# One hand-listed order for three batches of attention and two groups of the MLP, with casts of k on ScalarE

## The chip, the cores and the metric

The kernel runs on one core of a Trainium2 chip. The metric is the device time of one execution in microseconds (us).

## The reference

```python
def _attn_ref(q, k, v):                      # q, k, v: (8, 12, 448, 64) float32
    scores = (1 / sqrt(64)) * q @ k^T
    attn = np.maximum(scores, 0.0) ** 2 / S
    return attn @ v

def _moe_ref(x, w_in, w_out):                # x: 3584 x 768 = attention's output
    h = x @ w_in                             # 768 x 2048
    g = h * (1.0 / (1.0 + np.exp(-1.702 * h)))
    return g @ w_out                         # 2048 x 768
```

## The kernel before

Four heads of one batch are a unit u (three units a batch, 24 in all). One score step makes a 128 x 896 block in PSUM (the memory that TensorE's products are written to, here used in eight banks), ScalarE takes the relu, VectorE squares it; seven steps later an attention product uses the squares and VectorE evicts it into x transposed (xt). Tokens are taken in eight groups; m1 is one product of a group with 128 columns of w_in (six matmuls, followed by the gelu on ScalarE and a cast on GpSimd), m2 is a plain product with w_out. From group 1 on, products with w_out are made in pairs of token blocks from sums of the operands (seven products in place of eight); the sums of w_out that this needs are made once, on VectorE.

```python
    def relu2(u, j, sc):
        rl = rlp.tile([128, 2, S], F16, name="rl", tag="rl")
        at = atp.tile([128, 2, S], F16, name="at", tag="at")
        if NP <= u < 2 * NP and j == 3:
            nc.vector.tensor_scalar(out=rl, in0=sc[:, :, 0:S], scalar1=0.0, ..., op0=ALU.max)
        else:
            nc.scalar.activation(out=rl, in_=sc[:, :, 0:S], func=AF.Relu)
        if defer[0]:
            pend.append((at, rl))            # squared later, one per m1 or pair (flush)
        else:
            nc.vector.tensor_tensor(out=at, in0=rl, in1=rl, op=ALU.mult)
        return at
    ...
        # pair(): a product's bank "op", and its eviction
        elif n == 1:
            product(A[1][1], w_c, op)
            evac(eb, op, None)                                   # ScalarE
            nc.vector.tensor_tensor(out=ec, in0=ea, in1=eb, op=ALU.add)
        elif n == 2:
            product(sums[5], wout[1][1], op)
            evac(o0[:, hi], op, ea)                              # VectorE, frees the bank
            nc.vector.tensor_tensor(out=ea, in0=ec, in1=o0[:, hi], op=ALU.subtract)
    ...
        for f in range(NF):                  # group 0
            m1(0, f)
            ...
            if f % 2 == 1 or f > 12:
                visit(min(3, b1 - pos[0]))   # three steps: scores, or an attention product
        ...
            while prepped[0] < min(NU, upto_prep):
                cast(prepped[0], "k", nc.vector)
                cast(prepped[0], "q", nc.gpsimd)
                trans(prepped[0])
        ...
        for m in range(gblk[0] // 2):
            m2(0, m, 0)
            ...
            for i in range(4):               # four sums of w_out after each m2
                ...
                weight_sum(o, x, y, op, i, nc.vector)
```

All products and the sums' evictions share two PSUM banks (the other six hold scores and attention products), so a bank whose eviction is late stops TensorE two products on (for 1.43 us at 129.45 us, the longest such wait of the kernel before).

## Time and profile before

| | kernel before |
|---|---|
| time, median of 4 (range) | 399.82 us (399.57 to 400.13) |
| span of the profiled execution | 398.7 us |
| first product of group 0 (f0) starts | 30.41 us |
| first product of group 2 (g2) starts | 113.42 us |

The two marks cut the kernel where the argument needs it: up to f0 there is attention of batch 0 alone, between f0 and g2 lies what the list orders, and after g2 both kernels run the same schedule, whose casts and pair evictions the change alters. In all views PE is TensorE, PEld its weight loads, DVE VectorE, ACT ScalarE and POOL GpSimd; L292 is line 292 of that kernel, and `ht<-xt,win` reads output<-inputs. The marks can be read off TensorE's timeline (start, duration, engine, line, operation, output and inputs, shape, count):

```profile
30.41 0.82 PE L292 MATMUL ht<-xt,win 128*128 128x384 f16 x4
...
113.42 2.12 PE L292 MATMUL ht<-xt,win 128*128 128x384 f16 x12
```

The page's first part gives each engine's busy us, share and instructions. TensorE's 94% makes it the bound, but not evenly, as the stretches in the prediction show.

```profile
PE 372.9 (94%) x3104; PEld 194.0 (49%) x3104; DVE 267.6 (67%) x429; ACT 216.4 (54%) x317; POOL 145.0 (36%) x200
```

### The profile page before, as it was taken

To read this page: it belongs to the slowest core of one execution; us is meant where nothing else is said; L and a number is where in the kernel's file an instruction comes from. 1 tells how busy PE (TensorE), PEld (TensorE's weight loads), DVE (VectorE), ACT (ScalarE), POOL (GpSimd) and SP (SyncE) were. 2 spreads that over 40 slices of the span, in tenths; PEclk is the share of its full clock that TensorE was granted. 3 is DMA by queue.
4 is the path that set the end of the run, shared out by engine and by line. 5 is a ranking of instruction groups with operands and counts; after the bars stand their busy time and mean duration, and the time that the engine had idled before them with its cause. 6 is when DMAs were issued, how large, how long until landed. Compare 5 with 4: busy or idle time off the path is not lost.

```text
span 398.7 us, 7806 instructions
## 1 busy us (share of the span) xinstructions
PE 372.9 (94%) x3104; PEld 194.0 (49%) x3104; DVE 267.6 (67%) x429; ACT 216.4 (54%) x317; POOL 145.0 (36%) x200
## 2 busy tenths in 40 slices
PE   6588999999998999999999998999999999999994
PEld 3343545344454555454455554454545555554552
DVE  2886676678879688576877778566767765124484
ACT  3885671477775465666565564466666651232200
POOL 8444425534566142332453142333332222223100
PEclk9969999999999999999999999999999999999999
DMA  8999996999696725992969644971240111210323
GB/s 122 197 205 205 204 274 133 231 181 216 137 193 106 206 45 147 224 141 62 150 156 147 169 100 88 221 172 52 49 102 24 41 39 26 55 42 0 79 81 80
DMA packets 65222, 50.85 MB, mean 128 GB/s; under 512 B 35745, under 2 KB 61729, under 8 KB 65185
## 3 DMA queue, kind: packets, MB, share of 16 engines
q1 hardware_dynamic: 47872, 35.70, 38.2%
q0 software_dynamic: 17152, 14.55, 24.6%
q8 instruction: 24, 0.39, 0.4%
q10 hardware_dynamic: 160, 0.10, 0.1%
q14 instruction: 14, 0.11, 0.1%
HBM read 45.61 MB, written 11.01 MB: 142 GB/s over the span
## 4 chain that ended last, share of the span: by engine, by line
PE 68%; DVE 17%; ACT 5%; issue 4%; DMA 3%; POOL 1%; SPq 0%; DVEq 0%; ACTq 0%; POOLq 0%
PE ht L292 28%; PE op L358 24%; PE av L181 7%; PE sc L143 7%; ACT rl L157 4%; DVE at L171 3%; DVE osb L369 3%; PE op L319 3%; DVE at L161 2%; DVE k L104 2%; DMA qst<-in_q_dram 1%; DVE gt L353 1%; DVE wsum L343 1%; DMA q<-in_q_dram 1%; DVE as L353 1%
## 5 line engine op out<-in xcount | busy, mean ns | idle before, releaser
L299 POOL TENSOR_SCALAR gt<-gf 128x384 f16<-128x384 f32 (+1 forms) x128 | 90.8, 710 | 212.1 <-ACT gf L297 210.2
L157 ACT ACTIVATE rl<-sc 128x896 f16<-128x896 f32 x165 | 146.1, 920 | 37.3 <-PE sc L143 34.1
L292 PE MATMUL ht<-xt,win 128*128 128x384 f16 (+1 forms) x768 | 162.2, 353 | 2.9 <-DVE xt L198 1.0
L297 ACT ACTIVATE gf<-ht 128x384 f32<-128x384 f32 (+1 forms) x128 | 70.0, 547 | 114.5 <-PE ht L292 105.8
L292 PEld LDWEIGHTS <-win 128*128 128x128 f16 x768 | 71.8, 98 | 76.9 <-issue 16.5
L171 DVE TENSOR_TENSOR at<-rl 128x896 f16<-128x896 f16 x126 | 81.2, 670 | 13.6 <-ACT rl L157 13.3
L143 PE MATMUL sc<-qT,kT 64*64 64x448 f16 x672 | 49.4, 365 | 8.4 <-DVE qT L133 3.3
L358 PEld LDWEIGHTS <-gt 128*128 128x128 f16 x408 | 39.1, 98 | 33.0 <-issue 7.2
L358 PEld LDWEIGHTS <-as 128*128 128x128 f16 x312 | 30.1, 98 | 23.9 <-issue 3.8
L358 PE MATMUL op<-wout,as 128*128 128x384 f16 x224 | 40.7, 326 | 0.8 <-DVE osb L369 0.8
L358 PE MATMUL op<-wsum,gt 128*128 128x384 f16 x224 | 40.7, 326 | 0.3 <-ACT gf L297 0.3
L181 PE MATMUL av<-at,v 64*64 64x448 f16 x672 | 38.0, 360 | 3.0 <-DVE at L171 2.0
L143 PEld LDWEIGHTS <-kT 64*64 64x64 f16 x672 | 18.2, 106 | 34.7 <-issue 23.2
L358 PE MATMUL op<-wout,gt 128*128 128x384 f16 (+1 forms) x184 | 32.4, 319 | 2.7 <-DVE osb L369 2.1
L198 DVE CAST xt<-av 128x768 f16<-128x768 f32 (+2 forms) x36 | 26.9, 776 | 11.1 <-PE av L181 11.0
L161 DVE TENSOR_TENSOR at<-rl 128x896 f16<-128x896 f16 x42 | 25.9, 624 | 11.3 <-ACT rl L157 11.0
L181 PEld LDWEIGHTS <-v 64*64 64x64 f16 x672 | 20.7, 109 | 15.8 <-issue 5.4
L369 DVE SCALAR_TENSOR_TENSOR osb<-op,osb 128x384 f32<-128x384 f32 (+1 forms) x23 | 12.4, 541 | 23.3 <-PE op L358 23.0
L353 DVE TENSOR_TENSOR as<-gt 128x1024 f16<-128x1024 f16 x36 | 28.0, 804 | 0.0
L401 DVE TENSOR_TENSOR osb<-ea,eb 128x384 f32<-128x384 f32 x11 | 8.2, 743 | 23.7 <-ACT eb L367 23.7
L91 POOL DMA_DIRECT2D v<-in_v_dram x24 | 17.9, 745 | 8.4 <-DMA win<-in_moe_w_in_dram 2.9
L104 DVE CAST k<-kst 128x896 f16<-128x896 f32 x18 | 18.1, 1006 | 0.0
(38 smaller groups left out, 192.0 us busy)
## 6 DMA issues: line engine op xcount, KB each, us to landing
out_dram<-osb SPq DMA_DIRECT2D x54, 192.0 KB, 2.9
kst<-in_k_dram SPq DMA_DIRECT2D x18, 448.0 KB, 4.1
qst<-in_q_dram SPq DMA_DIRECT2D x18, 448.0 KB, 5.2
v<-in_v_dram POOLq DMA_DIRECT2D x24, 224.0 KB, 4.8
win<-in_moe_w_in_dram POOLq DMA_DIRECT2D x8, 384.0 KB, 11.3
wout<-in_moe_w_out_dram POOLq DMA_DIRECT2D x4, 768.0 KB, 11.7
k<-in_k_dram POOLq DMA_DIRECT2D x6, 224.0 KB, 9.0
q<-in_q_dram POOLq DMA_DIRECT2D x6, 224.0 KB, 8.9
```

The lines of the kernel that those rows point to most:

```text
L104: eng.tensor_copy(out=o, in_=i)
L143: nc.tensor.matmul(out=sc[c, a, 0:S], lhsT=st["kT"][r, j, c], rhs=st["qT"][r, :, c], start=True, stop=True)
L157: nc.scalar.activation(out=rl, in_=sc[:, :, 0:S], func=AF.Relu)
L161: nc.vector.tensor_tensor(out=at, in0=rl, in1=rl, op=ALU.mult)
L171: nc.vector.tensor_tensor(out=at, in0=rl, in1=rl, op=ALU.mult)
L181: nc.tensor.matmul(out=st["av"][64 * a:64 * a + 64, s, 0:S], lhsT=st["v16"][r, a, 64 * j:64 * j + 64], rhs=at[r, a, :], start=(j == 0), st ...
L198: nc.vector.tensor_copy(out=xts[g][:, 2 * pr:2 * pr + 2, 64 * (lo - gcum[g]):64 * (hi - gcum[g])], in_=av[:, :, 64 * (lo - b * J):64 * (hi ...
L292: nc.tensor.matmul(out=ht[:, 0:n], lhsT=w[:, kk, fo:fo + 128], rhs=xts[g][:, kk, 0:n], start=(kk == 0), stop=(kk == NK - 1))
L297: nc.scalar.activation(out=gf[:, 0:n], in_=ht[:, 0:n], func=AF.Gelu_apprx_sigmoid, scale=1.0 / SC)
L299: nc.gpsimd.tensor_scalar(out=gts[g][:, f, 0:n], in0=gf[:, 0:n], scalar1=SC, scalar2=1.0, op0=ALU.mult, op1=ALU.mult)
L353: nc.vector.tensor_tensor(out=out_, in0=x, in1=y, op=op)
L358: nc.tensor.matmul(out=op[:, 0:cw], lhsT=lhs[:, f, :], rhs=w[:, f, c0:c0 + cw], start=(start and f == 0), stop=(stop and f == HF - 1))
```

## The change

The loops that built the first 113 us are replaced by one list of words: `s3.4` is a score step, `a3` an attention product, `f0` and `F0` products of groups 0 and 1, `m0`, `n0` the two halves of group 0's output products, `e2` "square until two are left", `B2`, `A2` ... single sums of w_out, `K6`, `Q6`, `R6` casts and transposes, `L6`, `W6` loads, `d` a relu on VectorE, `h` one held until the next product. Batch 0's first attention product goes to the two product banks. Casts of k move from VectorE to ScalarE everywhere. In the pairs, three sums made from SBUF give way to two second evictions of the same bank.

```diff
-            t, u, j = items[pos[0]]
 ...
+        words = (
+            "e2 e1 s0.0 s0.1 e0 q1 s0.2 e1 s0.3 s0.4 k1 e2 e2 s0.5 k2 e0 e0 s0.6 s1.0 a0m "
 ... (13 lines cut)
+            "D2 e3 e0 e0 e2 F14 D3 e1 D1 e0 F15 e1 W12 e0 e0 L12").split()
 ...
-                cast(prepped[0], "k", nc.vector)
+                cast(prepped[0], "k", nc.scalar)
 ...
-            nc.vector.tensor_tensor(out=ec, in0=ea, in1=eb, op=ALU.add)
         elif n == 2:
             product(sums[5], wout[1][1], op)
             evac(o0[:, hi], op, ea)
-            nc.vector.tensor_tensor(out=ea, in0=ec, in1=o0[:, hi], op=ALU.subtract)
+            evac(o0[:, lo], op, eb, sc=-1.0 / SC)
         elif n == 3:
             product(sums[2], wout[0][0], op)
             evac(o1[:, lo], op, eb)
-            nc.vector.tensor_tensor(out=eb, in0=ec, in1=o1[:, lo], op=ALU.subtract)
+            evac(o1[:, hi], op, ea, sc=-1.0 / SC)
```

## The prediction

Its sum stands at 2.0 + 4.8 + 2.5 = 9.3 us, with the 0.83 us for a cast of k on ScalarE estimated from five relus of the kernel before (4.16 us). Where the text speaks of contention, the trace of the kernel before has four sums at 3.42 us beside a cast of q on GpSimd and the next four, without one, at 1.95, and three squares at 3.54 us from 104.44 us, beside casts on GpSimd, but three at 1.69 from 86.14 us, with nothing on GpSimd. Four more sums took 1.95 us from 72.94 us beside GpSimd's casts of the gelu, so not every operation there goes with longer times; that GpSimd is the cause was the author's reading.

> **What bounds the kernel now.** I read the stretches first, to see which engine is full when, then TensorE's timeline with its gaps, then the chain of work around single gaps, then the durations by form. The first view gives, for each stretch in us from the start of the span, busy us (and instruction counts) of TensorE, its weight loads, VectorE, ScalarE and GpSimd, the granted clock, the DMA share and GB/s.
>
> ```profile
> core 0: us, PE busy (x) PEld busy (x) DVE busy (x) ACT busy (x) POOL busy (x), PEclk, DMA share, GB/s
> 4.00:30.40 26.40, 18.96 (x290) 10.02 (x288) 19.64 (x34) 19.17 (x23) 16.07 (x24) 0.87 1.24 198
> 30.40:62.70 32.30, 28.69 (x316) 14.55 (x313) 21.73 (x33) 20.59 (x32) 12.14 (x20) 1.00 1.17 218
> 62.70:77.00 14.30, 13.39 (x74) 6.93 (x71) 10.14 (x18) 2.28 (x4) 8.63 (x9) 1.00 0.95 177
> 77.00:113.40 36.40, 35.14 (x313) 16.36 (x312) 25.95 (x39) 27.32 (x38) 18.05 (x23) 1.00 0.89 187
> 113.40:335.00 221.60, 216.35 (x1793) 113.78 (x1790) 163.14 (x257) 132.19 (x197) 76.31 (x100) 1.00 0.55 115
> 335.00:393.00 58.00, 57.14 (x323) 31.12 (x321) 26.36 (x48) 13.36 (x24) 10.94 (x18) 1.00 0.18 48
> ```
>
> The first row is attention of batch 0 alone: no product of group 0 can start before it, and TensorE is 72% busy there. The next three rows are group 0, then its first output products beside the sums of w_out, then group 1. ScalarE works 2.28 us in the 14.3 us of the third: no scores are made there, so it stands still while VectorE makes sums. From 113.4 us on TensorE is 98% busy. The kernel is therefore TensorE-bound from 30 us on; what can be won is TensorE's idle time (7.4 us before 30.4, 5.7 from there to 113.4, 5.3 to 335) and work the pipeline does at a worse rate.
>
> TensorE's timeline after 113 us has six gaps of note; three of them, with the chain of work (start, length) ahead of one:
>
> ```profile
> 129.45 1.46 PE L358 MATMUL op<-wout,gt 128*128 128x384 f16 x8 [1.43 <-DVE osb L369]
> 193.12 1.46 PE L292 MATMUL ht<-xt,win 128*128 128x512 f16 x6 [0.55 <-DVE osb L369]
> 241.69 0.38 PE L181 MATMUL av<-at,v 64*64 64x448 f16 x4 [1.71 <-DVE at L171]
> ```
> ```profile
> 186.62 0.57 DVE osb L369
> ...
> 187.22 0.56 DVE ea L405
> 187.78 0.60 DVE as L353
> 188.38 1.48 DVE at L171 x2
> 189.86 1.79 DVE k L104
> 191.65 0.95 DVE at L171
> 192.60 0.48 DVE osb L369
> ```
>
> Here a PSUM bank waits for its eviction, which stands in VectorE's queue behind a sum for ea, two squares, and a cast of k that took 1.79 us. The six gaps are 0.29, 1.43, 0.53, 0.55, 0.28 and 1.71 us, 4.8 us together, and five of them have VectorE's backlog as their cause.
>
> [...]four sums of w_out beside a GpSimd cast of q took 3.42 us, the next four without one 1.95; the k cast is 0.61 us at its shortest and 1.01 on average. [...]The trace has 0.92 for the relu from PSUM, [...]back to back, five relus took 4.16 us, 0.83 each, so I count 0.83 of queue time. [...]TensorE was 38% busy from 16 to 20 us, and the granted clock was 0.50 from 20 to 26 us.
>
> **Part 1, batch 0 (start to f0, the first product of group 0).** Nothing is removed; the transposes come in another order, squares are placed singly, and the first attention product goes to the two product banks, so that it does not hold a score bank. ScalarE sets the pace: relus begin at 8.07 us, f0 needs 21 of them, 21 x 0.83 = 17.4, so 25.5 us, then a square (0.54 start to start), the last step of the attention product (0.4) and the larger eviction (0.7): 27.1 us at best. VectorE has 21 squares x 0.54, 8 copies x 0.54 and three evictions x 1.1 = 19.0 us from 6.1 us, so 25.1, just under it. Before, f0 began at 30.41, of which the half-clock stretch cost some (ScalarE idle 1.68 us ahead of 24.59). I take 28.4: a gain of **2.0 us**.
>
> **Part 2, f0 to the end of group 1.** TensorE's work in the new list, by start-to-start times of the timeline: 40 scores x 0.23 = 9.2, five attention products x 1.33 = 6.7, 16 of group 0 x 1.06 = 17.0, 16 of group 1 x 1.35 = 21.6, six output products x 2.69 = 16.1, three transposes x 0.6 = 1.8: 72.4 us. Before, from 30.41 to 113.42 us, there were six more scores (1.4), one more attention product (1.3) and one more transpose (0.6): 75.7 us of work in 83.0, so **7.3 us** lost. Work that the new list leaves for later is no gain. The others allow it: VectorE has 41 squares x 0.54 = 22.1, nine relus x 1.0 = 9.0 (three before; they relieve ScalarE), evictions 5 x 1.1 + 6 x 0.48 = 8.4, twenty sums x 0.48 = 9.6, three copies 1.6: 50.7 us, 70% of the stretch without contention, and five k casts (5.4 us before) are gone. ScalarE has 31 relus x 0.83 = 25.7, 16 gelus x 0.40 + 16 x 0.49 = 14.2, five casts x 0.83 = 4.2: 44.1 us, 61%. The 113 to 335 us stretch runs at 74% and 60% with 2.4% of idle TensorE time. A list fixed by hand meets durations that vary with contention, so I allow 2.5 us, 3.5%. Gain **4.8 us**.
>
> **Part 3, groups 2 to 7.** VectorE loses 13 casts x 0.98 = 12.7 us, and per pair three additions (0.74 + 0.57 + 0.56) for two evictions (2 x 0.55): 11 x 0.77 = 8.5 us. That is 21.2 of its 163 us before 335 us, most of it off the path; the path has the 4.8 us of gaps. ScalarE gains 13 x 0.83 = 10.8 us there, to 65%. The added evictions hold a bank about 0.5 us longer twice a pair, and a cast can stand before a gelu whose bank TensorE wants. I take half of the gaps: **2.5 us**. The tail after 335 us and the store at the end don't change.
>
> Sum: 2.0 + 4.8 + 2.5 = 9.3 us; 399.83 - 9.3 = **390.5 us**.
>
> **Rivals.** (a) The list's wins turn into new bank waits: with two product banks, any eviction or gelu placed behind two squares that contention stretches from 0.54 to over 1 us stops TensorE. For it: every gap seen is of that kind. Against: 70% load. Parts 1 and 2 would then give 2 us in all, and the time is 395 to 397. (b) ScalarE's queue becomes the bound: casts wait for k's DMA or sit before gelus. For it: [...]loads were held until buffers were free (the DMA queue waited 20.4 us for k casts before 120 us). Against: 61 to 65% load, loads well ahead of use. Part 3 would be zero or negative: 393 to 396. (c) Transfers bound the early part: the DMA share is 1.2 of 1.3 up to 60 us, and the order on the queues hardly changes. Against: no product waited for a weight, and w_out had landed by 49.5 us, 13 us before its use. The effect would be under 2 us. (d) All goes well: no half-clock stretch, 1 us of idle time in part 2, the gaps of part 3 gone: 3.3 + 6.3 + 4.5 gives 385.7.
>
> **Range and chances.** The limit for faster by over 2% is 391.8, just 1.3 us above the sum, so it is not far from even. Part 2 has the largest spread (1 to 7 us), parts 1 and 3 one of about 1.5 us each side. Weights of 0.15 on (a), 0.15 on (b), 0.2 on (d), the rest around 390.5, give 385.5 to 395.5 for 8 in 10, and 0.60 for faster, 0.38 for within 2%, 0.02 for slower: no step adds work to the bound engine.
>
> **What would show it.** Right: the first group product starts near 28.4 us; group 1's last product ends near 103 to 104 us; ScalarE has no long idle stretch between 60 and 77 us; [...]fewer TensorE gaps ahead of which VectorE's eviction stands. Wrong: a first group product later than 30 us (part 1), over 5 us of TensorE gaps between it and the end of group 1 (part 2), or new gaps after 113 us whose releaser is a gelu or a cast on ScalarE (part 3). A half-clock stretch in a new place could cost 2 to 3 us in any of them.

## The result, and the profile after

| | before | after |
|---|---|---|
| time, median of 4 (range) | 399.82 us (399.57 to 400.13) | 393.29 us (392.59 to 394.80) |
| profiled span | 398.7 us | 393.0 us |
| f0 starts | 30.41 us | 32.45 us |
| f0 to g2 | 83.01 us | 75.27 us |
| g2 to the end | 285.28 us | 285.30 us |

The ratio of the two is 0.9841, with a 95% interval of 0.9808 to 0.9874. Ratios here are the mean time of one kernel's fast runs over the mean of the other's of the same rounds, so they are not quite the ratio of the quoted medians. The change is an improvement, but under 2%. The profiled execution of the changed kernel is the slowest of its four (394.8 us), so its three stretches are one draw; the experiments show which of them repeat.

The same view of stretches as in the prediction (same columns), with borders at the matching events:

```profile
4.00:32.40 28.40, 21.16 (x304) 10.97 (x302) 20.24 (x37) 18.56 (x22) 17.05 (x25) 0.82 1.24 197
32.40:60.80 28.40, 27.79 (x302) 13.88 (x298) 22.04 (x33) 20.93 (x32) 11.72 (x19) 1.00 1.22 223
60.80:77.00 16.20, 16.20 (x105) 8.15 (x102) 10.54 (x18) 6.35 (x11) 6.08 (x9) 1.00 0.99 201
77.00:107.70 30.70, 30.70 (x273) 14.53 (x271) 26.25 (x40) 21.13 (x31) 15.22 (x21) 1.00 1.08 191
107.70:331.00 223.30, 219.66 (x1812) 114.35 (x1809) 147.96 (x237) 144.74 (x212) 75.99 (x104) 1.00 0.55 117
```

From 60.8 us to g2 TensorE is never idle, where the kernel before lost 0.9 us in 14.3 and 1.3 in 36.4. Before f0 it got slower, at a mean granted clock of 0.82 (0.87 before). After g2, VectorE works 15 us less than in the kernel before (147.96 against 163.14) and ScalarE 12.6 more, and g2 to the end is as long as it was. The marks, and the page's first part:

```profile
32.45 1.15 PE L292 MATMUL ht<-xt,win 128*128 128x384 f16 x6
...
107.72 2.22 PE L292 MATMUL ht<-xt,win 128*128 128x384 f16 x12
```
```profile
PE 374.2 (95%) x3104; PEld 193.5 (49%) x3104; DVE 251.9 (64%) x408; ACT 226.2 (58%) x329; POOL 139.5 (35%) x200
```

Who kept TensorE waiting after g2 is in the view of waits (engine and line that waited, for whom, us in total, times, longest). First the kernel before, then the changed one:

```profile
PE op L358 <- DVE osb L369: 2.4, 4, 1.4
PE av L181 <- DVE at L171: 1.7, 1, 1.7
```
```profile
PE ht L292 <- ACT gf L297: 1.3, 4, 0.3
PE op L359 <- DVE osb L370: 0.5, 1, 0.5
PE op L359 <- ACT ea L368: 0.4, 1, 0.4
```

The long waits for VectorE are gone. In their place stand short ones for ScalarE: for the gelu (gf) and for a copy (ea). So two questions are open: why batch 0 came late, and why 15 us less work on VectorE bought nothing after g2.

### The profile page after: what moved, and what is told of

Its sections match the earlier page's. It is cut to its first block, busy times and chain, and to the rows that moved or that the text cites. A ratio compares the mean times of both kernels' runs of the same rounds, so it can differ in the third digit from the quotient of the medians.

```text
span 393.0 us, 7814 instructions
## 1 busy us (share of the span) xinstructions
PE 374.2 (95%) x3104; PEld 193.5 (49%) x3104; DVE 251.9 (64%) x408; ACT 226.2 (58%) x329; POOL 139.5 (35%) x200
## 4 chain that ended last, share of the span: by engine, by line
PE 78%; DVE 7%; ACT 7%; issue 4%; DMA 2%; POOL 1%; ACTq 0%; POOLq 0%
PE ht L292 32%; PE op L359 26%; PE sc L143 8%; PE av L183 7%; PE op L320 4%; ACT rl L157 4%; DVE osb L370 3%; DVE at L171 2%; DMA q<-in_q_dram 1%; ACT k L102 1%; ACT gf L297 1%; PE tr L129 1%; DMA out_dram<-osb 1%; DVE xt L203 0%; ACT eb L368 0%
## 5 line engine op out<-in xcount | busy, mean ns | idle before, releaser
L157 ACT ACTIVATE rl<-sc 128x896 f16<-128x896 f32 x159 | 140.7, 921 | 41.0 <-PE sc L143 40.0
L299 POOL TENSOR_SCALAR gt<-gf 128x384 f16<-128x384 f32 (+1 forms) x128 | 86.1, 673 | 209.2 <-ACT gf L297 208.4
L171 DVE TENSOR_TENSOR at<-rl 128x896 f16<-128x896 f16 x168 | 113.2, 698 | 22.3 <-ACT rl L157 22.0
L370 DVE SCALAR_TENSOR_TENSOR osb<-op,osb 128x384 f32<-128x384 f32 (+1 forms) x45 | 23.6, 545 | 27.1 <-PE op L359 26.9
L203 DVE CAST xt<-av 128x896 f16<-128x896 f32 (+2 forms) x34 | 25.8, 785 | 19.2 <-PE av L183 19.2
L183 PE MATMUL av<-at,v 64*64 64x448 f16 x644 | 36.2, 359 | 0.7 <-ACT rl L157 0.4
L370 DVE SCALAR_TENSOR_TENSOR osb<-op,ea 128x384 f32<-128x384 f32 x22 | 12.1, 552 | 24.7 <-PE op L359 13.4
L104 POOL CAST q<-qst 128x896 f16<-128x896 f32 x18 | 17.2, 954 | 0.3
L102 ACT ACTIVATE k<-kst 128x896 f16<-128x896 f32 x18 | 17.2, 958 | 0.0
```

The lines of the kernel that those rows point to most:

```text
L102: eng.activation(out=o, in_=i, func=AF.Copy)
L183: nc.tensor.matmul(out=st["av"][s][64 * a:64 * a + 64, 0:S], lhsT=st["v16"][r, a, 64 * j:64 * j + 64], rhs=at[r, a, :], start=(j == 0), st ...
L203: nc.vector.tensor_copy(out=xts[g][:, 2 * pr:2 * pr + 2, c], in_=st["pair"][:, :, f])
L299: nc.gpsimd.tensor_scalar(out=gts[g][:, f, 0:n], in0=gf[:, 0:n], scalar1=SC, scalar2=1.0, op0=ALU.mult, op1=ALU.mult)
L370: nc.vector.scalar_tensor_tensor(out=o, in0=op[:, 0:w], scalar=sc, in1=add, op0=ALU.mult, op1=ALU.add)
```

## The experiments

Every kernel below gave the right result. "List" is f0 to g2, "rest" g2 to the end, from the profile of one execution each; in the changed kernel and its relatives these two lengths repeat within 0.3 us where the code for them is the same (list 75.25 to 75.28 in the ten profiles where it is unchanged or only its sums are in bursts; rest 285.09 to 285.31 in the five with the changed code, 283.17 to 283.38 in the five with the later casts of k on VectorE). The kernel before is the exception: its rest took 285.28 us in one profile and 284.30 in before_fill, with the same code there. Nearly all of that is one wait of TensorE, first in the kernel before, then in before_fill, behind a sum (`as`) on VectorE:

```profile
124.88 1.99 DVE L353 TENSOR_TENSOR as<-gt 128x1024 f16<-128x1024 f16 x1
```
```profile
125.29 0.68 DVE L353 TENSOR_TENSOR as<-gt 128x1024 f16<-128x1024 f16 x1
...
128.87 1.46 PE L358 MATMUL op<-wout,gt 128*128 128x384 f16 x8 [0.24 <-DVE osb L369]
```

The same wait is 1.43 us in the kernel before, at 129.45 us. So where a kernel has one profile only (oldpair_fill, kvec_oldpair_fill, list_eager, list_kvec), a difference of 0.5 us is larger than the usual spread, but one wait that comes in some profiles only can make 1 us. The start of f0 and the total vary between executions anyway.

| kernel | f0 | list | rest | median (range) | ratio to before, 95% interval |
|---|---|---|---|---|---|
| after_fill | 30.08 | 75.25 | 285.14 | 392.88 (392.25 to 393.48) | 0.9856, 0.9834 to 0.9878 |
| before_fill | 31.01 | 82.98 | 284.30 | 399.82 (398.40 to 400.79) | 1.0019, 0.9998 to 1.0040 |
| order0 | 33.99 | 75.25 | 285.09 | 394.69 (393.55 to 396.11) | 0.9898, 0.9873 to 0.9922 |
| order0_fill | 30.11 | 75.28 | 285.27 | 393.09 (392.29 to 394.62) | 0.9862, 0.9839 to 0.9885 |
| after_again | 32.32 | 75.28 | 285.31 | 394.61 (394.21 to 395.32) | 0.9877, 0.9861 to 0.9893 |
| kvec_fill | 31.26 | 75.26 | 283.38 | 391.56 (391.27 to 392.02) | 0.9800, 0.9785 to 0.9814 |
| oldpair_fill | 32.45 | 75.26 | 285.61 | 394.59 (392.68 to 395.72) | 0.9867, 0.9842 to 0.9892 |
| kvec_oldpair_fill | 30.21 | 75.28 | 284.11 | 392.38 (391.38 to 393.18) | 0.9818, 0.9798 to 0.9838 |
| list_eager | 30.81 | 76.98 | 283.23 | 392.92 (392.53 to 393.94) | 0.9836, 0.9810 to 0.9861 |
| list_burst | 31.42 | 75.27 | 283.33 | 391.87 (391.44 to 393.14) | 0.9812, 0.9786 to 0.9837 |
| list_kvec | 30.31 | 75.99 | 283.23 | 393.54 (391.13 to 393.82) | 0.9836, 0.9805 to 0.9868 |
| kvec_warm | 31.87 | 75.25 | 283.17 | 390.97 (390.57 to 392.13) | 0.9781, 0.9744 to 0.9817 |

The first four ran on one chip, the next four on a second, the next three on it too, the last on a third. The kernel before had a median of 399.07 on the first and 399.65 to 399.76 on the others.

### Batch 0: half clock, or the order?

My theory was the half clock. Before f0 the granted clock was half for 6.83 us and again for 3.41 in the changed kernel's profile, in the kernel before once for 6.83. In the changed kernel's profile the record of the clock begins at 5.09 us, and it changes at 8.51, 15.33, 22.16 and 25.57 us, so its pieces up to there last 3.41 us or twice that. That too little work on TensorE brings the half clock was my supposition; to give TensorE more work without changing the order, I issued each score product of batch 0 twice, in both kernels:

```diff
-        for s in range(2):
+        for s in (0, 1, 0, 1) if u < NP else (0, 1):
```

> The changed kernel, with each score product of batch 0 issued twice (same result, 21 x 0.19 us more TensorE work in a stretch where TensorE is about 30% idle). Theory H, half clock: batch 0 came late in the changed kernel (group 0 starts at 32.45 us, before 30.41)[...]. Then the doubled work keeps the granted clock at 1.00 up to 40 us, group 0 starts by 30.0 us, the time is 390 to 391 us and the spread between executions (2.2 us now) shrinks below 0.6. Rival O, order: the new order of batch 0 is itself slower, by its late transposes; then group 0 still starts after 31 us and the time is 393 or more.

> The kernel before, with the same doubling. Theory H: its one half-clock stretch (19.4 to 26.2 us) goes too, group 0 starts at about 29 us and the time falls by 1 to 2 us, to 398 to 399. Rival O: the clock matters little, as ScalarE paces batch 0: no change, 399.8, or slower by up to 1 us for the added work.

The rival was that the new order of batch 0 is slower by itself. So I put the order of the kernel before into the list (each transpose where it was, each square straight after its relu, no attention product in the product banks), with and without the doubling:

```diff
-            "e2 e1 s0.0 s0.1 e0 q1 s0.2 e1 s0.3 s0.4 k1 ... e3 e0 a2 "
+            "s0.0 k1 e0 s0.1 q1 e0 s0.2 e0 s0.3 e0 l0 ... s3.0 l3 e0 a2 "
```

> The changed kernel with the order of batch 0 (scores, transposes, attention products, squares) as the kernel before has it, the rest of the list untouched. Theory H: [...]one half-clock stretch rather than two gives about 2 us less than the changed kernel, 391 to 392, with group 0 at 30 to 31 us. Rival O: the same gain, so this run alone does not tell them apart; the doubled one does. If neither holds, 393.3 or slower.

> As order0, with the doubled score products. Theory H: without half clock the two orders of batch 0 are within 0.5 us of each other, or the new one is the faster by up to 1.5 us. Rival O: this one is faster than after_fill by 1.5 us or more.

Two stretches of the changed kernel, then the first of them in after_fill (columns as in the stretches above; the granted clock is the third number from the end):

```profile
8.50:15.30 6.80, 6.08 (x78) 3.56 (x82) 4.47 (x8) 5.05 (x7) 4.74 (x7) 0.50 1.22 190
22.10:25.60 3.50, 3.07 (x36) 1.47 (x33) 2.30 (x5) 2.18 (x3) 1.42 (x3) 0.51 1.25 207
```
```profile
8.50:15.30 6.80, 5.92 (x121) 3.36 (x122) 5.67 (x10) 6.52 (x8) 4.75 (x7) 1.00 1.23 193
```

With the doubled products the clock stays at 1.00, ScalarE does 6.52 us of work in that stretch in place of 5.05, and f0 comes at 30.08 rather than 32.45: 2.4 us for this pair of profiles. List and rest differ by less than 0.2 us between the two. The rival falls: at full clock the two orders bring f0 at 30.08 and 30.11 in one profile each, with medians of 392.88 and 393.09, so no gain or loss of the order shows. (Both carry 21 x 0.19 us of added products, so 30.1 need not be what the full clock alone would give.)

But the expectation for the times was only partly met. The spread of after_fill is 1.23 us, not under 0.6, its median is 392.88, not 390 to 391, and doubling did nothing for the kernel before, which my theory said would gain 1 to 2 us.

Nor does the doubling always hold the clock: before_fill, kvec_fill and list_burst each have one half-clock stretch of 3.41 us, from 7.64, 7.95 and 8.15 us on, and f0 at 31.01, 31.26 and 31.42; the five doubled kernels of the table without one in their record, leaving out oldpair_fill and kvec_warm, have f0 at 30.08 to 30.81. The first piece of the start the doubling does not reach at all (in after_fill the first score product starts at 7.57 us). And the supposition behind it was not shown: TensorE was busy for 36% of the 3.41 us ahead of the drop in the kernel before, for 51% and 56% ahead of the two drops in the changed kernel, but for 60% of a stretch of after_fill (5.03 to 8.44 us) and 54% of one of kvec_warm (10.22 to 13.63 us) that no drop followed, so the busy share alone does not tell them apart. order0's time was missed too, 394.69 in place of 391 to 392.

In order0's profile the 14 matmuls of a transpose took 0.96 us up to 17 us, against 0.58 at full clock, so it was still at half clock there. The clock's record begins only at 20.7 us there (at 5.09 us in the changed kernel's profile); the view of stretches gives 1.00 up to that point, and the mean granted clock of that execution, 0.994, leaves the slow stretch out. (In oldpair_fill, with f0 at 32.45, the record begins only at 13.32 us, with transposes at 0.96 us ahead of it.) So a high mean clock in the list of runs does not mark a quick execution: order0's took 396.11 us at 0.994 and 393.55 at 0.989. It also means that order0 against after_again is no test of the order; only the two doubled kernels are.

> The changed kernel unchanged, as the base on this chip. Half clock decides its spread: executions with a mean granted clock of 0.992 and more near 0.982 of the kernel before, those at 0.985 about 1.3 us slower. If instead its mean equals that of after_fill (0.9856 of before), the half-clock stretches cost nothing on average, though the two profiles differ by 2.5 us.

The changed kernel again had f0 late (32.32 us), and its four executions were at 394.21 to 395.32 with clocks of 0.983 to 0.990. The expectation that 0.992 and 0.985 would separate could not be tried, as no execution had 0.992. Its ratio, 0.9877, is close to after_fill's 0.9856 on another chip, with overlapping intervals. So the half clock goes with the late f0 of these profiles (kvec_warm, below, is one with another cause); what it costs on average over executions stays open.

Why did f0 not come at 28.4 us, even at full clock? ScalarE's timeline in after_fill shows it (in brackets the idle time ahead and what ended it):

```profile
16.06 1.73 ACT L157 ACTIVATE rl<-sc 128x896 f16<-128x896 f32 x2 [0.71 <-PE sc L143]
...
24.08 4.96 ACT L157 ACTIVATE rl<-sc 128x896 f16<-128x896 f32 x6 [1.02 <-PE sc L143]
30.20 0.92 ACT L157 ACTIVATE rl<-sc 128x896 f16<-128x896 f32 x1 [1.16 <-PE sc L143]
```

Each of these gaps lies where TensorE has an attention product of 28 matmuls (1.3 us at full clock), and in the last two a transpose (0.58 us) as well, ahead of the next scores. ScalarE runs dry there once for each unit. The last gap falls at f0 itself and delays only what follows. VectorE has its share too: the chain of work that leads to f0, from 5 to 31 us, runs through VectorE's squares for 28.5% of its length and through relus for 17.3%, so ScalarE alone does not set the pace. No run here takes the two apart.

### After g2: what took the gain?

The base is after_fill. One kernel has the casts of k after the list back on VectorE, one the old pair evictions, one both:

```diff
-                cast(prepped[0], "k", nc.scalar)
+                cast(prepped[0], "k", nc.vector)
```

> after_fill with the 13 casts of k after the list put back on VectorE. After the list (from the first product of group 2 to the end) after_fill takes 285.2 us. Theory S, swap: the casts on ScalarE took away TensorE's long waits for VectorE but gave about 3 us of short waits for gelu and for the copies of ea; then the waits for ScalarE vanish here, waits for VectorE come back, and the stretch stays within 1.2 us of 285.2. Rival V: relieving VectorE was a gain of 2 us or more that something else ate; then this is slower by 2 us or more, 287 to 288.

> after_fill with the old evictions of the pairs: one eviction of a bank and a sum from SBUF in place of two evictions. Theory Hold: the second eviction keeps the bank 0.3 us longer than TensorE can wait, about eight times after the list; then those waits of 0.3 us go, the stretch shortens by 1 to 2.5 us to 283 to 284, though VectorE works 8.5 us more. Rival L, load: VectorE's added work costs as much in longer waits; then 285 or more.

> Both put back, so that only the list (and the doubled scores) differs from the kernel before. Theory S with Hold: the stretch after the list takes 285 to 287 us, with waits for VectorE of about 5 us as in the kernel before, and the whole is within 1.5 us of after_fill: nearly all of the change's gain is the list. Rival V: 288 us or more, the gain falling to below 4.5 us.

The rest takes 285.14 us with both parts of the change, 283.38 without the casts on ScalarE, 285.61 without the new evictions, 284.11 without either. So the move of the casts costs 1.8 us with the new evictions (285.14 - 283.38) and 1.5 with the old ones (285.61 - 284.11). The first stands on five profiles against five (285.09 to 285.31 against 283.17 to 283.38), among them after_again on the chip of kvec_fill. That is against all the theories: both S ("within 1.2 us") and V ("a gain") are wrong, and V has the wrong sign. The new evictions gain 0.5 us with the casts on ScalarE and 0.7 without (one profile each, so the size is uncertain; up to TensorE's last product it is 0.3 and 1.0, and the difference lies in the final store). Theory Hold falls too: no gain came of the old form, and rival L's bound of 285 us holds. The guess for both together, 285 to 287 us, was too long; that the whole stays within 1.5 us of after_fill came true (spans of 389.6 and 390.5). Timed in the same rounds, kvec_fill is at 0.9800 and after_again at 0.9877, with intervals far apart. Part of that is f0, which came 1.1 us earlier in kvec_fill; 1.8 us is the casts.

The mechanism can be seen around one product. First ScalarE in the changed kernel, with TensorE's product that waited for it:

```profile
145.04 1.73 ACT L157 ACTIVATE rl<-sc 128x896 f16<-128x896 f32 x2 [1.38 <-PE sc L143]
146.65 0.95 ACT L102 ACTIVATE k<-kst 128x896 f16<-128x896 f32 x1
147.49 0.49 ACT L297 ACTIVATE gf<-ht 128x384 f32<-128x384 f32 x1
...
148.04 1.14 PE L292 MATMUL ht<-xt,win 128*128 128x384 f16 x6 [0.29 <-ACT gf L297]
```

Then the same place in kvec_fill, where nothing stands between the relus and the gelu:

```profile
143.93 1.73 ACT L157 ACTIVATE rl<-sc 128x896 f16<-128x896 f32 x2 [1.37 <-PE sc L143]
145.54 0.50 ACT L297 ACTIVATE gf<-ht 128x384 f32<-128x384 f32 x1
```

In the changed kernel the gelu, which frees one of the two product banks, stands behind a cast that nothing needs for a long time, 0.84 us start to start. TensorE's next product wants that bank and waits. The loss is larger than the wait shown: from the start of the product ahead (146.28 us) to this one are 1.76 us, in kvec_fill 1.30 (145.17 to 146.47). All six waits for ScalarE after g2 in the changed kernel, four for a gelu, one for a copy of ea and one for a relu, have a cast of k among the three ScalarE instructions up to the one waited for; so six of the 13 casts fell where TensorE had to wait. All waits of TensorE for ScalarE after g2 are gone in kvec_fill; for VectorE there remain 1.2 us in two waits by the view of waits, up to the last products of the tail.

One more reading: with only the list new (kvec_oldpair_fill) the rest takes 284.11 us. The kernel before takes 285.28 with three score steps less to do after g2 (27 were made after batch 1 by then, 24 in the changed kernel), some 0.7 us; so for the same work it would be 286.0, or 285.0 by before_fill. The same code is thus 0.9 to 1.9 us quicker behind the new list. The wait of 1.7 us at 241.69 us, which before_fill has too, is not there; the one of 1.43 us at 129.45 is in one of its two profiles only, as shown above. That the visits fall differently among the products may be the reason, and so may three sums of w_out that the kernel before still makes on VectorE after g2; no run here isolates it.

### Within the list: what made it 75.3 us?

Three parts of the change were undone one by one, on kvec_fill: squares made straight after their relu, the twelve sums into new buffers in bursts of four after each output product, the five casts of k on VectorE.

```diff
-        defer[0] = True          # list_eager: squares follow their relus
```
```diff
-            "... e2 m2 e2 m1 e2 F0 B2 W6 A2 C2 Q7 e1 K7 B1 F1 e1 C0 m0 ..."
+            "... e2 m2 B0 B1 B2 B3 e2 m1 A0 A1 A2 A3 e2 F0 W6 Q7 e1 K7 F1 e1 m0 C0 C1 C2 C3 ..."
```
```diff
-                cast(int(w), "k", nc.scalar)
+                cast(int(w), "k", nc.vector)
```

> kvec_fill with each square of the list made straight after its relu in VectorE's queue, instead of where the list places it. The list (first product of group 0 to the first of group 2) takes 75.26 us in kvec_fill, with 1.3 us of waits. Theory P, placing: the placing of squares is what keeps bank evictions from queueing behind squares that still wait for a relu; then TensorE's waits rise to 4 to 7 us and the list to 78 to 81 us. Rival R, room: filling TensorE's queue with scores during the output products is what gained, and VectorE at about 70% has room; then the list stays within 1.5 us of 75.3.

> kvec_fill with the twelve sums of w_out into new buffers in bursts of four after the three first output products, as the kernel before has them, instead of spread over the list. Theory P: a burst of four takes 2 to 3.4 us on VectorE and holds evictions and squares back; the list lengthens by 1 to 3 us. Rival R: TensorE has product work to fill that time; within 0.7 us.

> kvec_fill with the five casts of k inside the list on VectorE as well, so that none is on ScalarE. After the list the casts on ScalarE cost 1.9 us in 13. If the same holds within the list, it shortens by 0.3 to 0.8 us. If the list was made for them (its evictions placed for that load of VectorE), it lengthens by 0.5 to 2 us.

The list took 76.98, 75.27 and 75.99 us, against 75.26. Placing the squares is worth 1.7 us, spreading those sums nothing, and the casts on ScalarE 0.7 us inside the list: the opposite sign of what they do after it, and at the lower edge of the second guess. TensorE's longest waits in the list, in list_eager and then in list_kvec (beside one of 0.4 us for a copy of a transpose, which kvec_fill has too):

```profile
PE ht L292 <- DVE qT L133: 1.0, 1, 1.0
PE ht L292 <- ACT gf L297: 0.6, 1, 0.6
```
```profile
PE ht L292 <- DVE osb L326: 0.7, 1, 0.7
```

In list_kvec a cast of k on VectorE holds back one eviction of an output product, and that single wait is the whole difference. In list_eager the copy of a transpose out of a product bank stands behind two squares; there is a wait of 0.6 us for a gelu as well, and why it arises was not followed up. Theory P gets the mechanism but not the size (1.7 us, not 3 to 6); rival R's bound of 1.5 is slightly exceeded. The list of the changed kernel gains 6.4 us (the next section works it out); the squares and the casts, undone one at a time, make 2.4 of it. If such parts add up, 4 us are left, for the order of TensorE's own work, the nine relus on VectorE and whatever else the list moves; no run here takes these apart.

### One more version: more products of zeros at the start

kvec_fill with three products of zeros in TensorE's first idle gaps and one more at its start, meant to have the clock full early (that such products do this was my supposition):

```diff
-        for _ in range(8):
+        for _ in range(9):
 ...
         trans_pe(0, "k")
+        warm_up(1)               # matmul of zeros into an unused score bank
         trans_pe(0, "q")
+        warm_up(2)
```

> kvec_fill with four more products of zeros into an unused score bank in TensorE's first idle gaps (one more before the first transposes, one and two after them)[...]. Theory H: the clock is full from at the latest 8.1 us in every execution, group 0 starts at 30.0 to 30.6 us, the list takes 75.3 and the rest 283.3 us: a span of 389 us, 390.6 to 391.3 by the clock of the runs, with a spread below 0.6 us; about 0.978 of the kernel before. Rival: what varies between executions is something else; the spread stays above 1.2 us and the mean at 0.980 to 0.982.

It has the lowest ratio, 0.9781, and the lowest median, 390.97 us, against 399.76 in the same rounds. Its interval overlaps kvec_fill's, so that the warm-up itself gains is not shown; what is shown is that kvec_fill beats the changed kernel (0.9800 against 0.9877 in the same rounds). The median came out as expected, but the spread is 1.56 us, so the expectation on spread failed: in the profiled execution the clock is full from 6.8 us on (a transpose took 0.96 us at 5.18 us, 0.65 at 6.61 and 0.58 at 8.99), and f0 is still at 31.87, because TensorE waited 1.56 us at 13.53 for k of a later unit to land. The arrival of the first loads is thus a second source of spread.

## Why the prediction was right or wrong

The measured 393.29 us lies within 385.5 to 395.5, 2.8 us above the point; "within 2%", which came true, had a chance of 0.38, less than "faster". The sum had three terms: 2.0 + 4.8 + 2.5 = 9.3. In the profiles they measured as follows. Two of the three failed and one did better than said, so it is the width of the range, 10 us, that made the number come true, and not the sum.

**Part 1, batch 0, failed.** It said f0 at 28.4 us; it came at 32.45. The step that failed is "relus begin at 8.07 us, f0 needs 21 of them, 21 x 0.83": ScalarE is not fed without gaps; it stands idle for 2.0 us in three gaps before f0 in after_fill (0.71, 0.31 and 1.02), and VectorE's squares, which the prediction had "just under it", are on the chain as well. At full clock f0 stays at 30.1 in either order, so the term was worth some 0.3 us in these profiles. And the half clock, which the prediction named as a risk of 2 to 3 us in its last line, took 2.4 us in this profile. The measured term is -2.0 us.

**Part 2, the list, was right in direction and too small.** The allowance of 2.5 us of idle time was the mis-sized term. In the same terms as predicted: the kernel before took 83.0 us, of which 3 scores and one transpose (0.7 + 0.6) are done elsewhere in the changed kernel, so 81.7; the list took 75.27, a gain of 6.4 us in place of 4.8. TensorE has one wait in the list, 0.44 us. Of its stated signs, "ScalarE has no long idle stretch between 60 and 77 us" fails: it works 6.35 us in 16.2 there, against 2.28 in 14.3 before, but still stands idle for 6.58 us in one piece, where the kernel before had 8.79:

```profile
67.58 0.60 ACT L297 ACTIVATE gf<-ht 128x512 f32<-128x512 f32 x1 [6.58 <-PE ht L292]
```

TensorE did not wait in that stretch, so ScalarE's idle time there cost nothing; at most the 0.9 us that TensorE lost there in the kernel before could be won.

**Part 3, groups 2 to 7, failed in sign for its main item.** It said that relieving VectorE of k's casts and of the pair's sums wins half of the 4.8 us of gaps. Most of the gaps for VectorE did go. But the casts on ScalarE cost 1.5 to 1.8 us, through the rival (b) that the prediction had weighed at 0.15, and in the form it described: "a cast can stand before a gelu whose bank TensorE wants". The pair evictions gained 0.5 to 0.7, and what the new list leaves behind it 0.9 to 1.9. The sum, from 286.0 to 285.3, is 0.7 us in place of 2.5; by before_fill, from 285.0, it would be a loss of 0.3. The 4.8 us of gaps from which the prediction took half held the wait of 1.43 us that is 0.24 in before_fill. The wrong step is the argument from ScalarE's load: 65% busy says nothing on what one instruction of 0.84 us delays.

The measured terms make -2.0 + 6.4 + 0.7 = 5.1, and the 0.6 us of the transpose that moved ahead of f0, which the prediction's sum did not carry, gives the 5.7 us between the two profiled spans. The medians differ by 6.5, since the profiled execution was the slowest of four.

**The rivals.** (a), that the list's wins turn into bank waits, did not happen. (c), late transfers, did not bind the list; it showed only in the spread of f0. The 0.61 to 1.87 us that a k cast takes on VectorE in the kernel before were real, but mattered less than the place of the same cast in ScalarE's queue.

## What to carry to other kernels

Moving an instruction to a less loaded engine is judged by what it then stands in front of: ask which of that engine's instructions frees a buffer that the bound engine is about to want, and whether the moved one can be placed behind it. Five casts won 0.7 us where a list placed them, and 13 lost 1.8 where a loop dropped them in. When a profile's early part differs by a few microseconds, look at the granted clock and at the duration of one fixed small operation (a transpose here: 0.58 us, and 0.96 at half clock) before blaming the order, and cut the kernel at events that both versions share.
